# Attention output turned by VectorE block transposes and packed by SBUF transfers

## The chip, the core and the metric

The kernel runs on one core of a Trainium2 chip. The core has TensorE (PE in the profile, its weight loads PEld), VectorE (DVE), ScalarE (ACT), GpSimd (POOL) and SyncE (SP), which here issues every DMA. Each engine runs its own instruction list in order, and semaphores tie the lists together. The metric is device time of one execution in microseconds (us).

## What is computed

One transformer block on 2048 tokens of width 640, in bf16:

```python
def _A_ref(x, wqkv, wo):                       # 32 heads of 20 columns
    qkv = (x @ wqkv).reshape(B, S, 3, H, Dh).transpose(2, 0, 3, 1, 4)
    q, k, v = qkv[0], qkv[1], qkv[2]
    scores = einsum("bhqd,bhkd->bhqk", q, k) * (Dh ** -0.5)
    o = einsum("bhqk,bhkd->bhqd", softmax(scores), v)
    return o.transpose(0, 2, 1, 3).reshape(B, S, D) @ wo
def _B_ref(x, w_gate, w_up, w_down):           # Df = 1728
    return (gelu(x @ w_gate) * (x @ w_up)) @ w_down
h = x + _A_ref(layernorm(x), wqkv, wo)
out = h + _B_ref(layernorm(h), w_gate, w_up, w_down)
```

## The kernel before

**Tiles.** The scores are made as tiles of 128 keys by 512 columns of queries in PSUM, 2048 tiles in all. The four heads of one group `g` (there are eight groups) sit in the four 32-row strips of TensorE. A quad is the four heads' tiles of one place. ScalarE turns most tiles into probabilities with one exp over the two or three PSUM banks of a "unit" (`unit`, L1020; units take banks 0 to 2 and 3 to 4 in turn). VectorE makes the exps of the rest by integer arithmetic (`d_exp`, L979: four readings of a bank, L985, then four operations over the quad). `D_QUADS` (L400) says how many quads of each slot go to VectorE, 86 in all, and `D_LEAD` when. A VectorE tile gets its scores either in the third bank of a three-bank unit, which then leaves two banks to ScalarE (the slots in `DIN`, L369), or in a background bank (7 or 5). The loop at L912 to L931 cuts the tiles into units. Probabilities are kept in a ring of `PR + PR2` = 18 tiles.

**Slots and query chunks.** The queries are worked on in ranges `QR`: one of 512, six of 256, four of 128. A slot is one accumulation of P times V in PSUM bank 6, with 512 columns: one group of a 512 range, two groups of a 256 range, four of a 128 range. There are 33 slots; the first six are groups 0 to 5 of the first 512 queries, and groups 6 and 7 of these follow as two slots of 256.

**Epilogue.** At a slot's end `epilogue` (L1131) copies bank 6 to `osb` (L1137, which frees the bank), TensorE turns it with four fp32 transposes into a background bank (L1149), and VectorE takes the reciprocals of the row sums (L1156; the sum is a 21st column of V) and multiplies into `o_nat` (L1160), queries on partitions. When a query chunk has all eight groups, `post` (L1175) turns `o_nat` again into `oT` (columns on partitions): for chunks 0 to 2 (`PE_T` = 3) by five TensorE transposes per 128 queries and a VectorE copy (`transposes`, L670), for chunks 3 to 8 by a DMA transpose on SP's queue (`dma_transposes`, L686), for chunk 9, the tail, in two steps on TensorE. Then come the multiplication with `wo` (L1213), the residual (L1214), the second layernorm, written into `o_nat` and turned into `hnT`, and the gated MLP (`mms`, L1242; `down`, L1350) as background work beside the next slots.

**Order.** The program carries its own planner (`Sched`, L48). Every operation is given an engine, a duration, a latency to landing for DMAs, a priority, and its dependencies; `schedule` simulates the engines and so fixes the order of each instruction list. On the chip each list runs in exactly this order: an instruction whose semaphore is late holds all that stand behind it on its engine. The planner's costs are written beside each operation: a DMA transpose is put at 1.25 us of SP and `XP_LAT` = 4 us to landing. The `wo` multiplication has priority 1.9, behind score multiplications (0) and P times V (1), ahead of the epilogue (2) and the background (3).

Of the kernel before, what the change touches and what calls it, by code (L numbers as in the profile page):

```python
# [356 lines left out]
D = 640  # L357
# [10 lines left out]
FOUR = ()  # L368
DIN = (16, 17, 18, 20, 21, 22, 23, 24, 25, 26, 27, 28, 29, 31, 32)  # L369
PE_WARM = ((14, ()), (6, (('x', 2),)), (4, (('x', 4),)))  # L370
# [18 lines left out]
W_EARLY = 4  # L389
PE_T = 3  # L390
XP_LAT, XR_LAT, W_LAT = 4, 5, 4.0
# [3 lines left out]
P_TANH = -1  # L395
PR, PR2 = 12, 6
D_PRIO = 2
D_SPLIT = 2
D_LAG = 2
D_QUADS = (0, 1, 2, 3, 3, 2, 4, 3, 2, 2, 3, 4, 4, 0, 3, 3, 3, 3, 4, 4, 3, 3, 4, 2, 3, 2, 2, 3, 4, 3, 1, 2, 1)  # L400
D_FIRST, D_PART = 2, 0.8
D_LEAD = ((0, 0, 0, 0, 0, 0, 0, 0), (0, 12, 18, 13, 9, 15, 10, 12, 10, 12, 17, 17, 11, 22, 17, 4, 16, 10, 16, 16, 17, 8, 22, 23, 7))
T_DVE = (0, 1, 3, 5, 9, 10, 11, 12, 13, 14)
# [12 lines left out]
def bass_sequential_preLN__mha_block__glu_gated_geglu__prompt_kernel(  # L416
# [12 lines left out]
    with ExitStack() as es:  # L429
# [3 lines left out]
        def sb(name, shape, dt=BF16):  # L433
            return es.enter_context(nc.sbuf_tensor(name, shape, dt))
# [38 lines left out]
        rc = sb("rc", [128, 2, 16], FP32)  # L473
        o_nat = sb("o_nat", [128, 4, D])
        dvx = sb("dvx", [128, 2048])
# [46 lines left out]
        ka = carve(2048)  # L522
        pts2 = carve(PR2 * 512)
        zb = dvx[:, 0:1024].rearrange("p (i s) -> p i s", i=2)

# [605 lines left out]
        def epilogue(s_, bk, d_sums):  # L1131
            s = s_ % 2
            c, gs = slots[s_]
            nq = QR[c][1]
            nt = nq // 128
            nblk = len(gs) * nt
            op("dve", I("tensor_copy", osb[:, 0:128 * nblk], PS[:, 512 * 6:512 * 6 + 128 * nblk]), c_dve(128 * nblk), P_QK,  # L1137
               reads=[("O", s_)], writes=["osb"], rel=[bk], after=tuple(d_sums))
            end = s_ == len(slots) - 1
            p = P_END if end else P_EPI  # L1140
            b2 = Bank(*(ALLB if end else BGC[c]))
            key = ("bk", sc_id())
            aft = set()
            tb = rbase(c)
            for g in gs:
                for tt in range(nt):
                    aft.update(sc.rd.get(("on", g, tb + tt), ()))
            for tt in range(nblk):
                op("pe", lambda eng, tt=tt, o=128 * (tt % nt * len(gs) + tt // nt): eng.transpose(bank(b2)[:, o:o + 128],  # L1149
                                                          osb[:, tt * 128:(tt + 1) * 128], identf[:]),  # L1150
                   c_mm(128, 2.5), p, mode="full", reads=["osb", "identf"], writes=[key], acq=[b2] if tt == 0 else [],
                   after=tuple(aft) if tt == 0 else ())
# [3 lines left out]
            op("dve", lambda eng: eng.reciprocal(rcv, bv()[:, :, :, DH]), 0.17, min(p, sc.ev), reads=[key], writes=[("rc", s)])  # L1156
# [3 lines left out]
            op("dve", lambda eng: eng.tensor_tensor(  # L1160
                dst, src(), rcn.rearrange("p (t j) -> p t j", t=nt).unsqueeze(3).to_broadcast([128, nt, 4 * n, DH]), ALU.mult),
               c_dve(80 * nblk), min(p, sc.ev), reads=[key, ("rc", s)], writes=[("on", g, tb + tt) for g in gs for tt in range(nt)], rel=[b2])


        def prefetch(c):
# [9 lines left out]
        def post(c, first_banks, banks, tail):  # L1175
# [7 lines left out]
            for tt in range(tb, tb + nt):  # L1183
                t = q0 // 128 + tt - tb
                i = t % 2
                if tail:
                    for k, (a0, a1) in enumerate(((0, NA - 1), (NA - 1, NA))):
                        bk, key = Bank(*(first_banks if k else BGC[c + 1])), ("bk", sc_id())
                        on = [("on", g, tt) for g in range(NG) if 80 * g < 128 * a1 and 80 * g + 80 > 128 * a0]
                        for a in range(a0, a1):  # L1190
# [35 lines left out]
            for tt in range(tb, tb + nt):  # L1226
                t = q0 // 128 + tt - tb
                ln_apply("dve", h_sb[:, tt, :], o_nat[:, tt, :], [("on", g, tt) for g in range(NG)], t, [("h", tt, 0), ("h", tt, 1)], pd)
                if tail:
                    transposes(o_nat[:, tt, :], [("on", g, tt) for g in range(NG)], hnT[:, :, tt * 128:(tt + 1) * 128], ("hnT", tt),  # L1230
                               first_banks, p, "dve", after=first)
                else:
                    dma_transposes(o_nat[:, tt, :], [("on", g, tt) for g in range(NG)], hnT[:, :, tt * 128:(tt + 1) * 128], ("hnT", tt),
                                   after=first)
# [167 lines left out]
        ui = 0  # L1402
        for s_, (c, gs) in enumerate(slots):
            if s_ < 8:
                g = s_
# [69 lines left out]
```

## Time and profile before

| | |
|---|---|
| median of 3 runs | 864.09 us (863.56 to 864.12) |
| profiled execution, its own time | 863.64 us |
| its span, first to last instruction | 862.0 us |
| granted TensorE clock, mean | 0.996 |
| DMA over the span | 34.34 MB, 40 GB/s |
| POOL busy | 60.5 us |

The views used below are: the page's totals of each engine; groups of instructions by line and shape, with busy time and mean duration of one; the chain of work that ended last, in order of time (start, duration, what); the timeline (start, duration, engine, line, operation, output and inputs, count); the table by windows; and DMA issues with their duration on the queue (SPq) and their time to landing. L437 is a helper that many operations share; they are told apart by their tiles. `regw` and `rege` are two SBUF regions that hold different tensors at different times, `kt_all` the keys, `pts` and a part of `rege` the ring of probabilities. A group's mean duration includes a tail that the next instruction of the same engine overlaps; the step from start to start is shorter.

### The profile page before, as it was taken

To read this page: it belongs to the slowest core of one execution; us is meant where nothing else is said; L and a number is where in the kernel's file an instruction comes from. 1 tells how busy PE (TensorE), PEld (TensorE's weight loads), DVE (VectorE), ACT (ScalarE), POOL (GpSimd) and SP (SyncE) were. 2 spreads that over 40 slices of the span, in tenths; PEclk is the share of its full clock that TensorE was granted. 3 is DMA by queue.
4 is the path that set the end of the run, shared out by engine and by line. 5 is a ranking of instruction groups with operands and counts; after the bars stand their busy time and mean duration, and the time that the engine had idled before them with its cause. 6 is when DMAs were issued, how large, how long until landed. Compare 5 with 4: busy or idle time off the path is not lost.

```text
span 862.0 us, 31727 instructions
## 1 busy us (share of the span) xinstructions
PE 821.2 (95%) x14358; PEld 428.9 (50%) x14385; DVE 733.7 (85%) x1443; ACT 831.1 (96%) x822; POOL 60.5 (7%) x194
## 2 busy tenths in 40 slices
PE   7999999999999999999998999999989999999998
PEld 3443232234445444454454444445556666666777
DVE  7736779889888999878799999999798689997884
ACT  7899999999999999999999999999999999999991
POOL 6500000000030000010002000100001010010100
PEclk8999999999999999999999999999999999999999
DMA  8211112540432000010010000020101110110000
GB/s 274 80 32 53 39 48 57 151 116 24 128 106 48 2 2 24 12 17 10 25 18 17 2 10 24 18 17 2 33 19 17 35 19 5 27 26 19 11 4 25
DMA packets 38775, 34.34 MB, mean 40 GB/s; under 512 B 18261, under 2 KB 36801, under 8 KB 38641
## 3 DMA queue, kind: packets, MB, share of 16 engines
q1 hardware_dynamic: 38640, 32.32, 14.8%
q8 instruction: 113, 1.85, 0.9%
q14 instruction: 22, 0.17, 0.1%
HBM read 20.12 MB, written 8.09 MB: 33 GB/s over the span
## 4 chain that ended last, share of the span: by engine, by line
ACT 65%; PE 19%; DVE 13%; POOL 1%; issue 1%; DMA 1%; SPq 0%; POOLq 0%; ACTq 0%
ACT pts L437 42%; ACT rege L437 20%; PE ps L1044 5%; PE ps L437 3%; PE ps L1248 3%; DVE qt_all L985 3%; PE ps L1365 3%; DVE qt_all L437 2%; ACT qt_all L437 2%; PE ps L735 2%; DVE rege L985 2%; PE ps L730 1%; DVE rege L437 1%; DVE rege L1293 1%; DVE dvx L437 1%
## 5 line engine op out<-in xcount | busy, mean ns | idle before, releaser
L437 ACT ACTIVATE pts<-ps 128x1536 bf16<-128x1536 f32 (+1 forms) x480 | 549.8, 1289 | 2.7 <-PE ps L1044 2.1
L1044 PE MATMUL ps<-qt_all,kt_all 32*128 32x256 bf16 (+2 forms) x4736 | 316.4, 257 | 20.3 <-ACT pts L437 9.1
L437 ACT ACTIVATE rege<-ps 128x1536 bf16<-128x1536 f32 (+1 forms) x232 | 275.8, 1289 | 2.4 <-PE ps L437 1.5
L1044 PEld LDWEIGHTS ps<-qt_all,kt_all 32*128 32x128 bf16 x4736 | 118.0, 92 | 208.9 <-ACT pts L437 82.4
L1248 PE MATMUL ps<-rege,regw 128*128 128x256 bf16 (+1 forms) x1193 | 136.0, 251 | 2.2 <-DVE rege L985 1.0
L985 DVE TENSOR_SCALAR qt_all<-ps 128x512 int16<-128x512 f32 x176 | 118.4, 682 | 10.4 <-PE ps L1044 9.9
L985 DVE TENSOR_SCALAR rege<-ps 128x512 int16<-128x512 f32 x164 | 110.5, 683 | 19.5 <-PE ps L1044 19.0
L437 PE MATMUL ps<-pts,v_all 128*21 128x256 bf16 (+2 forms) x2656 | 119.8, 259 | 0.0
L1248 PEld LDWEIGHTS ps<-rege,regw 128*128 128x128 bf16 x1193 | 86.0, 98 | 37.1 <-issue 19.7
L437 PE MATMUL ps<-rege,v_all 128*21 128x256 bf16 (+2 forms) x1676 | 98.5, 267 | 0.2
L437 PEld LDWEIGHTS ps<-pts,v_all 128*21 128x21 bf16 x2656 | 57.9, 91 | 26.2 <-issue 21.2
L735 PE MATMUL ps<-regw 128*128 128x512 bf16 (+1 forms) x270 | 65.0, 348 | 3.3 <-issue 1.6
L1365 PE MATMUL ps<-regw,rege 128*128 128x320 bf16 x374 | 66.3, 301 | 0.7 <-DVE rege L1293 0.4
L437 PEld LDWEIGHTS ps<-rege,v_all 128*21 128x21 bf16 x1676 | 41.2, 91 | 23.6 <-issue 12.9
L437 DVE TENSOR_SCALAR qt_all<-qt_all 128x2048 int16<-128x2048 int16 (+2 forms) x103 | 47.8, 472 | 0.7
L1307 DVE SCALAR_TENSOR_TENSOR qt_all<-qt_all,ps 128x512 bf16<-128x512 f16 (+1 forms) x54 | 36.0, 667 | 12.2 <-PE ps L1248 8.2
L1365 PEld LDWEIGHTS ps<-regw,rege 128*128 128x128 bf16 x374 | 31.5, 98 | 22.5 <-issue 9.1
L437 POOL CAST mv<-mv 128x4 bf16<-128x4 f32 (+2 forms) x13 | 3.5, 271 | 545.8 <-DVE mv L437 543.5
L1293 DVE TENSOR_SCALAR rege<-ps 128x512 bf16<-128x512 f32 (+1 forms) x54 | 36.1, 668 | 5.6 <-PE ps L1248 3.4
L735 PEld LDWEIGHTS ps<-regw 128*128 128x128 bf16 x289 | 23.4, 99 | 29.9 <-issue 16.9
L437 DVE TENSOR_SCALAR rege<-rege 128x2048 int16<-128x2048 int16 x56 | 38.1, 683 | 0.3
L437 ACT ACTIVATE qt_all<-qt_all 128x512 f16<-128x512 f16 (+1 forms) x54 | 38.0, 727 | 0.0
(137 smaller groups left out, 840.6 us busy)
## 6 DMA issues: line engine op xcount, KB each, us to landing
q_rows<-regw SPq DMA_DIRECT2D x20, 128.0 KB, 2.0
out_dram<-rege SPq DMA_DIRECT2D x16, 160.0 KB, 2.7
regw<-in_A_wqkv_dram SPq DMA_DIRECT2D x3, 800.0 KB, 11.5
rege<-in_A_x_dram SPq DMA_DIRECT2D x7, 320.0 KB, 3.6
regw<-in_B_w_gate_dram SPq DMA_DIRECT2D x5, 432.0 KB, 3.4
regw<-in_B_w_up_dram SPq DMA_DIRECT2D x5, 432.0 KB, 3.4
rege<-in_A_x_dram SPq DMA_DIRECT2D x3, 640.0 KB, 6.9
kt_all<-k_rows SPq DMA_DIRECT2D x12, 160.0 KB
```

The lines of the kernel that those rows point to most:

```text
L437: return lambda eng: getattr(eng, method)(*args, **kwargs)
L730: return [lambda eng, j=j: eng.matmul(PS[32 * j:32 * j + 32, 512 * bk.b + lo:512 * bk.b + hi], l[:, 32 * j:32 * j + 32], r, start=start, s ...
L735: yield op("pe", lambda eng, l=l, r=r, k=k: eng.matmul(bank(bk, n), l, r, start=(k == 0), stop=(k == len(steps) - 1), skip_group_check=Tru ...
L985: d_ops.append(op("dve", lambda eng: eng.tensor_scalar(v[:, 512 * h:512 * h + 512], bank(b), EXP_MUL, 0.0, ALU.mult, ALU.max), c_dve(512), ...
L1044: return lambda eng: eng.matmul(out()[:, kk * nq:(kk + 1) * nq], kt_all[32 * j:32 * j + 32, g, kt * 128:(kt + 1) * 128], qt_all[32 * j:32 ...
L1248: op("pe", lambda eng, a=a, f=f, fi=fi: eng.matmul(bank(bk)[:, fi * nq:(fi + 1) * nq], w[:, a, F0[f]:F0[f] + 128], hnT[:, a, 128 * tb:128 ...
L1293: op("dve", lambda eng, bg=bg, fv=hv(k, w), w=w: eng.tensor_scalar(fv, bank(bg, w), 0.5, None, ALU.mult), c_dve(w), p, reads=[kg], writes= ...
L1307: op("dve", lambda eng, bu=bu, z=z, w=w: eng.scalar_tensor_tensor(out=z, in0=z.bitcast(F16), scalar=1.0, in1=bank(bu, w), op0=ALU.add, op1 ...
L1365: op("pe", lambda eng, f=f, o=o, hf=hf, bk=bk: eng.matmul(bank(bk, 320), ha_f[:, o:o + 128], wd[:, f, hf * 320:(hf + 1) * 320], start=(f = ...
```

## The change

In `epilogue`, for all ranges but the last of 128 queries, VectorE now reads bank 6 with a transpose in 32x32 blocks into `osb`, takes the reciprocals, multiplies into a new bf16 tile `onb`, and transposes that in blocks into the first half of `osb`, seen as bf16. Each head's 20 columns then stand on 20 partitions, and one DMA per head, from SBUF to SBUF on SP's queue, puts them at their place in `ox`, the memory of `o_nat` with the columns on partitions; a head that crosses a multiple of 128 takes two DMAs. `post` multiplies `ox` with `wo` without turning it first. The second layernorm is turned as before. `onb` takes one place of the ring of probabilities (`PR2` 6 to 5). The constants of the distribution, `D_QUADS`, `D_LEAD` and `DIN`, are new: 88 quads for VectorE, and 9 slots in `DIN` in place of 15. The planner is told `O_ISSUE` = 0.1 us of SP and `O_LAT` = 2.5 us to landing for each new DMA.

```diff
-DIN = (16, 17, 18, 20, 21, 22, 23, 24, 25, 26, 27, 28, 29, 31, 32)
+DIN = (7, 16, 22, 25, 26, 27, 28, 29, 30)
...
-PE_T = 3
+O_ISSUE, O_LAT = 0.1, 2.5
...
-PR, PR2 = 12, 6
+PR, PR2 = 12, 5
...
-D_QUADS = (0, 1, 2, 3, 3, 2, 4, 3, 2, 2, 3, 4, 4, 0, 3, 3, 3, 3, 4, 4, 3, 3, 4, 2, 3, 2, 2, 3, 4, 3, 1, 2, 1)
+D_QUADS = (0, 3, 2, 3, 3, 3, 3, 2, 2, 2, 3, 4, 3, 3, 3, 3, 3, 3, 4, 4, 2, 3, 4, 0, 4, 2, 3, 4, 2, 3, 1, 4, 0)
 D_FIRST, D_PART = 2, 0.8
-D_LEAD = ((0, 0, 0, 0, 0, 0, 0, 0), (0, 12, 18, 13, 9, 15, 10, 12, 10, 12, 17, 17, 11, 22, 17, 4, 16, 10, 16, 16, 17, 8, 22, 23, 7))
+D_LEAD = ((0, 0, 0, 0, 0, 0, 0, 0), (0, 10, 18, 12, 6, 11, 11, 18, 17, 10, 13, 16, 20, 16, 16, 5, 22, 23, 27, 7, 8, 9, 18, 30, 5))
...
-        o_nat = sb("o_nat", [128, 4, D])
+        ox = sb("ox", [128, 4 * D])
+        o_nat = ox[:, :].rearrange("p (t d) -> p t d", t=4)
...
         pts2 = carve(PR2 * 512)
+        onb = carve(512)
...
+            if c < len(QR) - 1:
+                n = len(gs)
+                w = 128 * nblk
+                o16 = osb[:, :].bitcast(BF16)
+                op("dve", I("transpose", osb[:, 0:w], PS[:, 512 * 6:512 * 6 + w]), c_dve(w), P_QK,
+                   reads=[("O", s_)], writes=["osb"], rel=[bk], after=tuple(d_sums))
+                ov = osb[:, 0:w].rearrange("p (k e) -> p k e", e=32)
+                rcn = rc[:, s, 0:w // 32]
+                op("dve", I("reciprocal", rcn, ov[:, :, DH]), 0.2, p, reads=["osb"], writes=[("rc", s)])
+                op("dve", I("tensor_tensor", onb[:, 0:w].rearrange("p (k e) -> p k e", e=32)[:, :, 0:DH], ov[:, :, 0:DH],
+                            rcn.unsqueeze(2).to_broadcast([128, w // 32, DH]), ALU.mult), c_dve(DH * w // 32), p, reads=["osb", ("rc", s)], writes=["onb"])
+                op("dve", I("transpose", o16[:, 0:w], onb[:, 0:w]), c_dve(w), p, reads=["onb"], writes=["osb"])
+                for gi, g in enumerate(gs):
+                    for j in range(4):
+                        r = 80 * g + DH * j
+                        k = 0
+                        while r < 80 * g + DH * j + DH:
+                            m = min(DH - k, 128 - r % 128)
+                            src = o16[32 * j + k:32 * j + k + m, nq * gi:nq * gi + nq]
+                            if nq > 256:
+                                dst = ox[r % 128:r % 128 + m, :].rearrange("p (u a s) -> p u a s", u=2, a=NA)[:, :, r // 128, :]
+                                src = src.rearrange("p (u s) -> p u s", u=2)
+                            else:
+                                dst = ox[r % 128:r % 128 + m, D * tb:D * (tb + nt)].rearrange("p (a s) -> p a s", a=NA)[:, r // 128, :]
+                            op("sp", I("dma_start", dst, src), O_ISSUE, P_EPI, reads=["osb"], writes=[("on", g, tb + tt, 2 * j + (k > 0)) for tt in range(nt)],
+                               sem="ot", lat=O_LAT)
+                            k += m
+                            r += m
+                return
...
-                elif c < PE_T:
-                    transposes(o_nat[:, tt, :], [("on", g, tt) for g in range(NG)], oT[:, :, tt * 128:(tt + 1) * 128],
-                               ("hnT", tt), first_banks, P_EPI, "dve", after=first)
-                else:
-                    dma_transposes(o_nat[:, tt, :], [("on", g, tt) for g in range(NG)], oT[:, :, tt * 128:(tt + 1) * 128],
-                                   ("hnT", tt), after=first)
...
-                    st = [(oT[:, a, tt * 128:(tt + 1) * 128], wo[:, a, hf * 320:(hf + 1) * 320]) for a in range(NA)]
+                    ot = oT if tail else ox[:, D * tb:D * (tb + nt)].rearrange("p (a s) -> p a s", a=NA)
+                    o = tt if tail else tt - tb
+                    st = [(ot[:, a, o * 128:(o + 1) * 128], wo[:, a, hf * 320:(hf + 1) * 320]) for a in range(NA)]
...
-                        list(chain(bk, key, 320, st, [("hnT", tt), "wo"], p, after=(sc.lw[("h", tt, hf)], *first)))
+                        list(chain(bk, key, 320, st, [k for t_ in range(tb, tb + nt) for k in onk(t_)] + ["wo"], p, after=(sc.lw[("h", tt, hf)], *first)))
...
+            if s_ == 0:
+                cst(I("memset", onb[:].bitcast(FP32), 0.0), "onb", 256, e_ops + q_first)
```

`onk(tt)` lists the keys of all eight groups and eight half-heads of one block of 128 queries, so each `wo` multiplication waits for every packing DMA of its chunk.

More of the change, by code (lines that the diff above doesn't have):

```diff
@@ L1136, in epilogue @@
             nblk = len(gs) * nt
+            end = s_ == len(slots) - 1
+            p = P_END if end else P_EPI
+            tb = rbase(c)
+            if c < len(QR) - 1:
[27 more added lines that the diff above has]
+                return
@@ L1137, in epilogue @@
             op("dve", I("tensor_copy", osb[:, 0:128 * nblk], PS[:, 512 * 6:512 * 6 + 128 * nblk]), c_dve(128 * nblk), P_QK,
                reads=[("O", s_)], writes=["osb"], rel=[bk], after=tuple(d_sums))
-            end = s_ == len(slots) - 1
-            p = P_END if end else P_EPI
             b2 = Bank(*(ALLB if end else BGC[c]))
@@ L1143, in epilogue @@
             aft = set()
-            tb = rbase(c)
             for g in gs:
                 for tt in range(nt):
-                    aft.update(sc.rd.get(("on", g, tb + tt), ()))
+                    for k in range(8):
+                        aft.update(sc.rd.get(("on", g, tb + tt, k), ()))
             for tt in range(nblk):
@@ L1161, in epilogue, with onk @@
                 dst, src(), rcn.rearrange("p (t j) -> p t j", t=nt).unsqueeze(3).to_broadcast([128, nt, 4 * n, DH]), ALU.mult),
-               c_dve(80 * nblk), min(p, sc.ev), reads=[key, ("rc", s)], writes=[("on", g, tb + tt) for g in gs for tt in range(nt)], rel=[b2])
+               c_dve(80 * nblk), min(p, sc.ev), reads=[key, ("rc", s)], writes=[("on", g, tb + tt, k) for g in gs for tt in range(nt) for k in range(8)], rel=[b2])
+        def onk(tt):
+            return [("on", g, tt, k) for g in range(NG) for k in range(8)]
         def prefetch(c):
@@ L1188, in post @@
                         bk, key = Bank(*(first_banks if k else BGC[c + 1])), ("bk", sc_id())
-                        on = [("on", g, tt) for g in range(NG) if 80 * g < 128 * a1 and 80 * g + 80 > 128 * a0]
+                        on = [("on", g, tt, k) for k in range(8) for g in range(NG) if 80 * g < 128 * a1 and 80 * g + 80 > 128 * a0]
                         for a in range(a0, a1):
@@ L1227, in post @@
                 t = q0 // 128 + tt - tb
-                ln_apply("dve", h_sb[:, tt, :], o_nat[:, tt, :], [("on", g, tt) for g in range(NG)], t, [("h", tt, 0), ("h", tt, 1)], pd)
+                ln_apply("dve", h_sb[:, tt, :], o_nat[:, tt, :], onk(tt), t, [("h", tt, 0), ("h", tt, 1)], pd)
                 if tail:
-                    transposes(o_nat[:, tt, :], [("on", g, tt) for g in range(NG)], hnT[:, :, tt * 128:(tt + 1) * 128], ("hnT", tt),
+                    transposes(o_nat[:, tt, :], onk(tt), hnT[:, :, tt * 128:(tt + 1) * 128], ("hnT", tt),
                                first_banks, p, "dve", after=first)
                 else:
-                    dma_transposes(o_nat[:, tt, :], [("on", g, tt) for g in range(NG)], hnT[:, :, tt * 128:(tt + 1) * 128], ("hnT", tt),
+                    dma_transposes(o_nat[:, tt, :], onk(tt), hnT[:, :, tt * 128:(tt + 1) * 128], ("hnT", tt),
                                    after=first)
```

## Prediction, made before the result was known

> **What bounds the kernel now.** I read the totals first, then the table by windows for the stage in which exps run, then the chain of work that ended last.
>
> ```profile
> span 862.0 us, 31727 instructions
> PE 821.2 (95%) x14358; PEld 428.9 (50%) x14385; DVE 733.7 (85%) x1443; ACT 831.1 (96%) x822; POOL 60.5 (7%) x194
> ACT 65%; PE 19%; DVE 13%; POOL 1%; issue 1%; DMA 1%; SPq 0%; POOLq 0%; ACTq 0%
> ```
>
> ```profile
> core 0: us, PE busy (x) PEld busy (x) DVE busy (x) ACT busy (x) POOL busy (x), PEclk, DMA share, GB/s
> 480.00:600.00 120.00, 115.38 (x1914) 56.80 (x1916) 118.86 (x226) 118.53 (x120) 4.25 (x14) 1.00 0.08 13
> ...
> 32.00:838.00 806.00, 773.87 (x13891) 396.62 (x13911) 697.85 (x1349) 801.55 (x766) 43.87 (x145) 1.00 0.14 34
> ```
>
> In the 806 us from the first exp to the last, ScalarE is idle for 4.45 us. So the time is ScalarE's work, with 32 us ahead of it and 24 us behind it. VectorE has 108 us of idle time there (806 - 698), though almost none between 480 and 600 (1.1 us of 120). TensorE's 774 us are pipelined and say little about room. The step of one exp is read from the chain, where consecutive pieces stand start to start (a three-bank exp takes 1.34 us, a two-bank one 0.92, a tanh of the MLP 0.51), and the counts from the groups by shape:
>
> ```profile
> 647.93 0.92 ACT rege L437
> 648.85 0.51 ACT qt_all L437
> 649.36 1.34 ACT rege L437
> ...
> L437 ACT ACTIVATE pts<-ps 128x1024 bf16<-128x1024 f32 x291 | 312.2, 1117 | 0.2 <-PE ps L437 0.2
> L437 ACT ACTIVATE pts<-ps 128x1536 bf16<-128x1536 f32 x189 | 293.6, 1554 | 2.5 <-PE ps L1044 2.1
> L437 ACT ACTIVATE rege<-ps 128x1024 bf16<-128x1024 f32 x141 | 152.1, 1117 | 1.5 <-PE ps L437 1.5
> L437 ACT ACTIVATE rege<-ps 128x1536 bf16<-128x1536 f32 x91 | 141.7, 1557 | 0.9 <-PE ps L1044 0.8
> ```
>
> That is 280 long exps (189 + 91) and 432 short ones (291 + 141), or 280 x 1.34 + 432 x 0.92 = 772.6 us; some 54 tanhs bring it near 800.
>
> **ScalarE's work.** The loop that cuts tiles into units, counted through with the old constants, gives just these 280 and 432. With the new quads, leads and `DIN` it gives 303 of three banks, 393 of two and one of a single bank (0.92 - 0.42 = 0.5 us): 406.0 + 361.6 + 0.5 = 768.1 us. ScalarE loses **4.5 us**: 3.4 us are the eight tiles of two more quads (0.42 to 0.43 each), the rest 15 fewer instructions. Since ScalarE is full, this comes off the end if nothing starves it.
>
> **TensorE and VectorE.** The rows that are removed or changed, and those that make up a quad:
>
> ```profile
> L1149 PE MATMUL ps<-identf,osb 128*128 128x128 f32 x128 | 26.2, 296 | 1.4 <-DVE rege L1293 1.0 <-DVE rege L781 0.2
> L674 PE MATMUL ps<-ident,o_nat 128*128 128x128 bf16 x35 | 3.3, 221 | 0.0
> ...
> L985 DVE TENSOR_SCALAR qt_all<-ps 128x512 int16<-128x512 f32 x176 | 118.4, 682 | 10.4 <-PE ps L1044 9.9
> L437 DVE TENSOR_SCALAR rege<-rege 128x2048 int16<-128x2048 int16 x56 | 38.1, 683 | 0.3
> L437 DVE TENSOR_TENSOR dwx<-qt_all,dwx 128x1024 bf16<-128x1024 bf16 x50 | 32.8, 678 | 0.2
> L437 DVE COPY osb<-ps 128x512 f32<-128x512 f32 x31 | 21.2, 684 | 4.1 <-PE ps L437 3.9
> L1160 DVE TENSOR_TENSOR o_nat<-ps,rc 128x320 bf16<-128x320 f32 x31 | 15.0, 484 | 0.4
> L1156 DVE RECIPROCAL rc<-ps 128x16 f32<-128x16 f32 x31 | 7.8, 251 | 6.1 <-PE ps L1149 6.1
> L683 DVE COPY rege<-ps 128x640 bf16<-128x640 bf16 x7 | 3.4, 484 | 1.4 <-PE ps L674 1.4
> ```
>
> Of the 33 slots 30 take the new path. TensorE loses 120 of the 128 fp32 transposes, 120/128 x 26.2 = 24.6 us, and 30 of the 35 small ones, 2.8 us. ScalarE waits for TensorE only in its 4 us, so I count this at nothing: room, not time.
>
> VectorE keeps a pass over bank 6 (now a transpose), the reciprocals and the multiplication, and adds a second transpose. No block transpose stands in this trace. By the nearest row, the copy of the same 512 columns, it takes 0.684 us; from below 0.42 us, by the bf16 operations on 512 columns, from above 1.37, twice the copy. I take 0.684, so 30 x 0.684 = 20.5 us are added. A quad is 4 x 0.682 + 2 x 0.683 + 2 x 0.678 = 5.45 us, two more are 10.9; six copies of 0.484 go, 2.9. VectorE gains 28.5 us against 108 idle. In the full stretch (480 to 600, slots 17 to 21) five transposes add 3.4 us, but the new `D_QUADS` has 16 quads there in place of 17, which takes 5.45 off. I count VectorE at nothing; without that cover it is a rival below. The shorter ring costs nothing by the same count of units: seven laps of 18 hold about 46 units (712 in 109 laps), of 17 about 44 (697 in 110), and ScalarE's waits for P times V are 1.7 us in all (the two "PE ps L437" above), which is the most I see this change by.
>
> **SP's queue, where the change is priced low.** The new path issues one DMA per head and a second where a head crosses a multiple of 128: 9 per slot of one or two groups, 18 per slot of four (12 once, 13 never; groups 0 to 5 of the first range make 27 in six slots). All in all 27 + 9 + 9 + 4 x 36 + 3 x 36 = 297. The planner believes 0.1 us of issue each and 2.5 us to landing. The trace has an operation of almost the same form, eight DMAs of 20 rows from SBUF to SBUF that place the keys of group 0 (`kt_all<-regw`), beside the same 20 rows fetched from DRAM:
>
> ```profile
> L437 SPq DMA_DIRECT2D kt_all<-k_rows x16: 292/330/338, 42.4 to 145.8; - x16
> L437 SPq DMA_DIRECT2D kt_all<-regw x8: 706/707/933, 22.8 to 28.2; - x8
> ...
> 22.75 6.20 SPq L437 DMA_DIRECT2D kt_all<-regw  x8
> ...
> k_rows<-regw SPq DMA_DIRECT2D x12, 128.0 KB, 1.8
> rege<-o_nat SPq DMA_TRANSPOSE x24, 2.9
> ```
>
> The columns of the first two rows are the shortest, median and longest issue in ns: 707 from SBUF to SBUF, 330 from DRAM. Eight took 6.20 us, 0.775 each. The price of the new DMAs lies between 0.1 (the planner's) and 0.775; I take 0.775, the row with the same memories on both sides and the same rows. To landing I take 1.8 us (between 1.8 and 2.9 in the rows above).
>
> The Trainium skill speaks for the change here: "DMA: Bandwidth & Descriptors", section "Issuing engines are not separate DMA queues", says that the sequencer's time to initiate a DMA is usually small relative to the DMA. By that, this part would cost nothing and the sum would be the 859 of the first rival. The row of 707 ns beside 1.8 us to landing speaks against it.
>
> **What it does to the order.** Most packing DMAs have a whole slot, some 25 us, to land. The last slot of a chunk hasn't: the chunk's `wo` multiplication waits for all of them, and in TensorE's list it stands where the planner thinks that they have landed. Before, the planner expected two DMA transposes after 2 x 1.25 + 4 = 6.5 us, one after 5.25. The trace shows `wo` that near behind them:
>
> ```profile
> 440.27 3.15 SPq L437 DMA_TRANSPOSE rege<-o_nat  x2
> 446.08 0.45 PE L735 MATMUL ps<-wo,rege 128*128 128x320 bf16 x2
> ...
> 688.36 1.21 SPq L437 DMA_TRANSPOSE rege<-o_nat  x1
> 695.40 0.57 PE L735 MATMUL ps<-wo,rege 128*128 128x320 bf16 x3
> ```
>
> So `wo` came 5.8 and 7.0 us after the first issue: 0.7 early and 1.8 late against the plan, 0.5 late on average. Now the plan expects 9 x 0.1 + 2.5 = 3.4 us for 9 DMAs and 4.3 for 18. At 0.775 the ninth is issued after 8 x 0.775 = 6.2 and lands at 8.0; the eighteenth after 13.2, landing at 15.0. `wo` waits 8.0 - 3.4 - 0.5 = **4.1 us** in six chunks (0 to 5) and 15.0 - 4.3 - 0.5 = **10.2 us** in three (6 to 8). Behind it on TensorE stand the next score multiplications, and ScalarE waits for these. It has between one short exp (0.92) and a pair (2.26) in hand, on average 1.6. It idles 2.5 us six times and 8.6 three times: 15.0 + 25.8 = **40.8 us**, which nothing makes good, because ScalarE has no slack later.
>
> **Sum.** The profiled execution took 863.64 us, 1.6 more than its span and 0.45 less than the median of the three runs. 863.6 - 4.5 + 40.8 = **900 us**. With the ends of slack and cover (1.8 and 2.26; 0 and 0.92) the idle is 6 x 0.5 + 3 x 6.6 = 23 or 6 x 3.7 + 3 x 9.8 = 52, so 882 to 911 for this case. A stall may also cost clock: between 16 and 20 us the trace grants 0.50, after a stretch in which TensorE was busy for 2.46 of 4 us.
>
> ```profile
> 12.00:16.00 4.00, 2.46 (x14) 1.22 (x15) 3.95 (x13) 3.40 (x9) 2.54 (x6) 0.66 1.07 363
> 16.00:20.00 4.00, 3.78 (x25) 2.84 (x25) 2.63 (x9) 2.12 (x5) 1.67 (x5) 0.50 0.83 280
> ```
>
> One such slice of 4 us at half clock behind each of the three long stalls is up to 2 us each; it moves the upper end to about 915. The Trainium skill, "TensorE: Matmul & The Clock Gate", Part 1, has the same halving after an idle window of about 3.4 us; by that page's window the estimate is 1.7 us each, 905 in sum.
>
> **The rivals.**
> - *The packing is hidden* (0.27): the DMAs issue fast, or land before the planner's moment, and ScalarE stays full. Then 863.6 - 4.5 = **859**, faster; 855 at best, if the 4.45 us of idle shrink because 27 us of TensorE work are gone. For it speaks that ScalarE's plan held so exactly; against it the 707 ns.
> - *The issue costs what the DRAM rows cost* (0.12): 0.33 with a gap of 0.04. Nine land after 8 x 0.37 + 1.8 = 4.8, 1.4 late, which ScalarE's reserve covers; eighteen after 8.1, 3.8 late, 1.7 us of idle after slack and cover, three times. 863.6 - 4.5 + 5.1 = **864**, no change.
> - *VectorE becomes the bound* (0.07): if a block transpose takes 1.37, the 60 of them add 30 x (0.69 + 1.37) = 62 us against 108, and in 480 to 600 five slots need 10.3 us where 1.1 + 5.45 are to be had. Some 4 us are lost there and as much in the other full slices: about **867**, slower. It decides from 1.3 us per transpose.
> - *The stalls* (0.54): **900**, the forecast.
>
> The range goes from 856 to 915. A measurement of this kernel can tell about 0.2% from no change. Faster 0.27, the same 0.12, slower 0.61.
>
> **What would show it.** Packing DMAs on SP's queue at about 0.7 us each; TensorE waiting for a DMA ahead of the first `wo` multiplication of chunks 0 to 8, about 4 us six times and 10 us three times; ScalarE idle by some 40 us between its first and last exp, in nine places, with 768 us of exps. If the new rows show 0.1 to 0.3 us, or the waits lie elsewhere, this is wrong. VectorE should show 30 x 2 transposes near 0.68 us and about 762 us busy.

## The result, and the profile after

The changed kernel takes **931.0 us** (median of 6 runs, 926.39 to 931.65), the kernel before 863.72 us (6 runs, 862.87 to 864.12). The ratio is 1.0771, with a 95% interval of 1.0749 to 1.0793: slower by 67 us. The forecast was 900 us, with a range up to 915. The sign and the kind of loss were right, the size was not.

The page's totals of the changed kernel, with the shares of the chain that ended last:

```profile
span 929.2 us, 31786 instructions
PE 830.0 (89%) x14242; PEld 422.6 (45%) x14242; DVE 753.9 (81%) x1483; ACT 829.9 (89%) x807; POOL 61.7 (7%) x195
ACT 35%; DVE 28%; PE 26%; SPq 6%; issue 2%; DMA 2%; POOL 1%; POOLq 0%; DVEq 0%; ACTq 0%
```

ScalarE has as much work as before (829.9 us against 831.1), but its share of the span falls from 96% to 89%, and in the chain ScalarE's 65% have become 35%. SP's queue, at 0% before, now holds 6% of the chain, and it is the queue of the new DMAs. VectorE's share of the chain rises too, from 13% to 28%; whether VectorE is the cause is tested in experiment 1. No engine has become fuller than ScalarE was, so the time is in waits. The table by windows says how much of it (columns: window, its length, busy time and instructions of PE, PEld, DVE, ACT and POOL, granted clock, DMA share, GB/s):

```profile
32.00:906.00 874.00, 783.40 (x13798) 391.93 (x13797) 718.27 (x1389) 799.27 (x750) 44.32 (x145) 0.96 0.13 32
217.00:232.00 15.00, 14.31 (x146) 5.44 (x146) 7.47 (x17) 10.74 (x10) 2.90 (x14) 0.80 0.08 28
360.00:372.00 12.00, 11.39 (x121) 4.17 (x120) 7.86 (x16) 8.34 (x7) 0.00 (x0) 0.59 0.01 1
740.00:748.00 8.00, 8.00 (x154) 4.97 (x152) 5.18 (x13) 3.95 (x4) 0.66 (x3) 0.67 0.02 4
799.01:802.35 3.34, 3.34 (x51) 1.97 (x52) 1.09 (x3) 0.00 (x0) 0.00 (x0) 0.50 0.02 5
```

From the first exp to the last ScalarE is idle for 874.0 - 799.27 = **74.7 us**; before it was 4.45. The phase is 68 us longer, the span 67.2. So the whole loss lies between the first and the last exp, and it is idle time of ScalarE. The other four rows are stretches behind waits of TensorE, and they come up again below: TensorE is busy in nearly all of each, at a granted clock of 0.50 to 0.80, and ScalarE still has gaps (in the last row it has not started again).

The new operations, in the tables by tile and by shape (DMA rows: shortest, median and longest time on the queue in ns):

```profile
L437 SPq DMA_DIRECT2D ox<-osb x297: 554/707/1337, 66.5 to 860.4; - x149
```

```profile
L437 ACT ACTIVATE pts<-ps 128x1536 bf16<-128x1536 f32 x199 | 303.5, 1525 | 11.9 <-PE ps L1046 11.6
L437 ACT ACTIVATE rege<-ps 128x1536 bf16<-128x1536 f32 x104 | 158.8, 1527 | 17.9 <-PE ps L1046 17.3 <-PE ps L437 0.3
L437 DVE STREAM_TRANSPOSE osb<-ps 128x512 f32<-128x512 f32 x30 | 21.3, 709 | 6.0 <-PE ps L437 4.6 <-PE ps L732 1.4
L437 DVE STREAM_TRANSPOSE osb<-rege 128x512 bf16<-128x512 bf16 x30 | 21.0, 701 | 0.0
```

There are 297 packing DMAs at a median of 707 ns of SP's queue, 303 exps of three banks (199 + 104), and 60 block transposes at 0.70 us, all as counted. The waits of TensorE by line (us in total, times, longest), with SP's queue and `wo` (L732 and L737) in them:

```profile
PE ps L737 <- DMA ox<-osb: 22.5, 4, 9.7
PE ps L737 <- issue: 12.4, 2, 8.7
PE ps L732 <- DMA ox<-osb: 10.0, 1, 10.0
PE ps L1279 <- DMA rege<-ox: 8.9, 2, 8.0
```

The first three rows are `wo` behind its packing DMAs. (The "issue" of the second row is no other cause: its 8.7 us end at 739.5, just after SP has issued the last packing DMA of chunk 6 at 738.3.) The last row isn't `wo`. It is the up and gate multiplication of the MLP, waiting for the second layernorm's DMA transposes, and the forecast doesn't have it. On ScalarE the stalls look so (timeline of ScalarE; in brackets the idle time ahead of the instruction):

```profile
219.77 1.45 ACT L437 ACTIVATE rege<-ps 128x1536 bf16<-128x1536 f32 x1 [5.62 <-PE ps L1046]
223.73 5.55 ACT L437 ACTIVATE pts<-ps 128x1024 bf16<-128x1024 f32 x5 [1.17 <-PE ps L1046]
...
256.23 1.02 ACT L437 ACTIVATE rege<-ps 128x1024 bf16<-128x1024 f32 x1 [3.27 <-PE ps L1046]
360.04 1.02 ACT L437 ACTIVATE rege<-ps 128x1024 bf16<-128x1024 f32 x1 [1.27 <-PE ps L1046]
362.29 2.52 ACT L437 ACTIVATE pts<-ps 128x1536 bf16<-128x1536 f32 x2 [1.23 <-PE ps L1046]
...
466.12 1.02 ACT L437 ACTIVATE pts<-ps 128x1024 bf16<-128x1024 f32 x1 [4.28 <-PE ps L1046]
568.88 1.45 ACT L437 ACTIVATE pts<-ps 128x1536 bf16<-128x1536 f32 x1 [4.81 <-PE ps L1046]
...
709.15 1.45 ACT L437 ACTIVATE rege<-ps 128x1536 bf16<-128x1536 f32 x1 [8.23 <-PE ps L1046]
742.01 1.02 ACT L437 ACTIVATE rege<-ps 128x1024 bf16<-128x1024 f32 x1 [8.80 <-PE ps L1046]
744.38 1.45 ACT L437 ACTIVATE rege<-ps 128x1536 bf16<-128x1536 f32 x1 [1.34 <-PE ps L1046]
802.35 1.02 ACT L437 ACTIVATE pts<-ps 128x1024 bf16<-128x1024 f32 x1 [11.05 <-PE ps L1046]
...
863.26 1.02 ACT L437 ACTIVATE pts<-ps 128x1024 bf16<-128x1024 f32 x1 [9.97 <-PE ps L1046]
```

This gives the account of the 74.7 us:

| place | ScalarE idle, us | forecast |
|---|---|---|
| `wo` of chunks 0 to 4 (5.62, 3.27, 1.27, 4.28, 4.81); chunk 5 shows none | 19.3 | 15.0 |
| `wo` of chunks 6 to 8 (8.80, 11.05, 9.97) | 29.8 | 25.8 |
| the layernorm's transposes of chunk 5, at 709 | 8.2 | not in it |
| eight gaps of 0.9 to 1.3 in the 10 us behind the stalls (1.17, 1.23 and 1.34 above) | 9.3 | in the upper end only |
| all the rest (4.5 before the change) | 8.1 | 4.5 |
| sum | 74.7 | 45.3 |

One long `wo` stall (chunk 7) and the stall that was not forecast, in the timeline of all engines:

```profile
690.38 13.28 SPq L437 DMA_DIRECT2D ox<-osb  x18
692.49 0.81 DVE L437 TENSOR_SCALAR ox<-rege,mu,rs 128x640 bf16<-128x640 bf16 x2
703.70 2.57 SPq L437 DMA_TRANSPOSE rege<-ox  x2
707.77 0.80 PE L1279 MATMUL ps<-rege,regw 128*128 128x256 bf16 x3 [8.04 <-DMA rege<-ox]
...
784.64 13.23 SPq L437 DMA_DIRECT2D ox<-osb  x18
...
799.01 1.52 PE L737 MATMUL ps<-wo,ox 128*128 128x320 bf16 x5 [9.74 <-DMA ox<-osb]
800.73 0.61 PE L437 MATMUL ps<-qt_all,v_all 128*21 128x128 bf16 x16
801.12 0.64 PE L437 MATMUL ps<-dvx,v_all 128*21 128x128 bf16 x16
801.69 0.61 PE L1046 MATMUL ps<-qt_all,kt_all 32*128 32x128 bf16 x12
```

At 784.64 the eighteen DMAs of the chunk's last slot start and hold SP for 13.23 us, 0.735 each. TensorE stands at `wo` from 789.3, 4.6 us after the first issue, to 799.01. At 692.5 it is another queue: the layernorm of chunk 5 is ready by 693.3, but its two DMA transposes stand on SP behind the 18 packing DMAs of chunk 6's first slot. They start at 703.70, and the MLP that waits for them holds up TensorE and, by 8.23 us, ScalarE.

### The profile page after: what moved, and what is told of

It reads as the page before. It is cut to its first block, busy times and chain, and to the rows that moved or that the text cites. A ratio compares the mean times of both kernels' runs of the same rounds, so it can differ in the third digit from the quotient of the medians.

```text
span 929.2 us, 31786 instructions
## 1 busy us (share of the span) xinstructions
PE 830.0 (89%) x14242; PEld 422.6 (45%) x14242; DVE 753.9 (81%) x1483; ACT 829.9 (89%) x807; POOL 61.7 (7%) x195
## 4 chain that ended last, share of the span: by engine, by line
ACT 35%; DVE 28%; PE 26%; SPq 6%; issue 2%; DMA 2%; POOL 1%; POOLq 0%; DVEq 0%; ACTq 0%
ACT pts L437 23%; ACT rege L437 11%; PE ps L1046 7%; DVE qt_all L987 6%; SPq L437 6%; PE ps L437 5%; DVE qt_all L437 5%; PE ps L737 4%; PE ps L1279 4%; DVE rege L437 3%; DVE dvx L987 3%; PE ps L1396 3%; DVE dwx L437 3%; DVE osb L437 2%; DVE rege L1324 2%
## 5 line engine op out<-in xcount | busy, mean ns | idle before, releaser
L1046 PE MATMUL ps<-qt_all,kt_all 32*128 32x256 bf16 (+2 forms) x4736 | 323.6, 261 | 25.2 <-ACT pts L437 6.8
L437 ACT ACTIVATE rege<-ps 128x1536 bf16<-128x1536 f32 (+1 forms) x220 | 268.2, 1303 | 32.2 <-PE ps L1046 31.7
L1279 PE MATMUL ps<-rege,regw 128*128 128x256 bf16 (+1 forms) x1179 | 136.7, 253 | 12.5 <-DMA rege<-ox 8.9
L1279 PEld LDWEIGHTS ps<-rege,regw 128*128 128x128 bf16 x1179 | 86.1, 98 | 51.8 <-issue 30.3
L987 DVE TENSOR_SCALAR dvx<-ps 128x512 int16<-128x512 f32 x100 | 67.3, 680 | 8.4 <-PE ps L1046 8.0
L737 PE MATMUL ps<-regw 128*128 128x512 bf16 (+1 forms) x297 | 70.5, 350 | 1.4 <-DVE regw L685 0.9
L737 PE MATMUL ps<-wo,ox 128*128 128x320 bf16 x130 | 32.9, 386 | 37.9 <-DMA ox<-osb 22.5
L1245 DVE TENSOR_TENSOR rege<-ps,rege 128x320 bf16<-128x320 f32 x32 | 15.4, 486 | 60.5 <-PE ps L737 56.2
L1396 PE MATMUL ps<-regw,rege 128*128 128x320 bf16 x350 | 63.1, 302 | 0.8 <-DVE dvx L987 0.8
L987 DVE TENSOR_SCALAR rege<-ps 128x512 int16<-128x512 f32 x72 | 48.5, 681 | 7.4 <-PE ps L1046 7.0
L437 DVE TENSOR_SCALAR qt_all<-qt_all 128x512 f16<-128x512 f16 (+2 forms) x111 | 52.6, 484 | 0.4
L1396 PEld LDWEIGHTS ps<-regw,rege 128*128 128x128 bf16 x350 | 28.2, 98 | 22.4 <-issue 8.2
```

Of the source, the lines that this page charges most:

```text
L437: return lambda eng: getattr(eng, method)(*args, **kwargs)
L737: yield op("pe", lambda eng, l=l, r=r, k=k: eng.matmul(bank(bk, n), l, r, start=(k == 0), stop=(k == len(steps) - 1), skip_group_check=Tru ...
L987: d_ops.append(op("dve", lambda eng: eng.tensor_scalar(v[:, 512 * h:512 * h + 512], bank(b), EXP_MUL, 0.0, ALU.mult, ALU.max), c_dve(512), ...
L1046: return lambda eng: eng.matmul(out()[:, kk * nq:(kk + 1) * nq], kt_all[32 * j:32 * j + 32, g, kt * 128:(kt + 1) * 128], qt_all[32 * j:32 ...
L1279: op("pe", lambda eng, a=a, f=f, fi=fi: eng.matmul(bank(bk)[:, fi * nq:(fi + 1) * nq], w[:, a, F0[f]:F0[f] + 128], hnT[:, a, 128 * tb:128 ...
L1396: op("pe", lambda eng, f=f, o=o, hf=hf, bk=bk: eng.matmul(bank(bk, 320), ha_f[:, o:o + 128], wd[:, f, hf * 320:(hf + 1) * 320], start=(f = ...
```

## The experiments

The theory after the result: the time is lost because the planner is told 0.1 us for a DMA that holds SP's queue for 0.71 us, and so puts `wo` and the layernorm's consumers too early. The rival causes are the block transposes on VectorE, a landing time that is too long whatever the planner knows, and the new constants. Each kernel was timed beside the kernel before, whose medians were 863.4 to 863.7 us. In the edits that follow, everything else is as in the changed kernel unless said otherwise.

**1. Tell the planner the issue.**

```diff
-O_ISSUE, O_LAT = 0.1, 2.5
+O_ISSUE, O_LAT = 0.75, 2.5
```

> The changed kernel with one constant altered: the planner is told 0.75 us of SP per packing DMA in place of 0.1. Theory A (the loss is the order: `wo` and the layernorm's transposes stand too early in the lists, because each packing DMA holds SP for 0.71 us): the waits of TensorE for ox shrink below 1 us each, ScalarE's idle time between its first and last exp falls from 75 us to 5 to 14, and the time is 859 to 869 us. Theory B (the loss is the work itself, 297 small transfers and some 20 us more of VectorE): telling the planner only moves the waits, and the time stays above 900.

868.26 us (866.84 to 869.26), ratio 1.0054 (1.0039 to 1.0069). One number that only the planner reads takes away 63 of the 67 us; the same DMAs and the same transposes run.

```profile
32.00:838.00 806.00, 760.92 (x13779) 384.50 (x13801) 717.11 (x1381) 797.39 (x750) 48.36 (x146) 1.00 0.13 35
```

In that kernel's table by windows ScalarE is idle for 8.6 us of 806 (7.1 between its first and last exp) and the clock is 1.00. VectorE has as much work as in the changed kernel (717 us against 718 in the two windows) and yet the 63 us are gone, so it isn't their cause.

**2. Tell only a late landing**, which keeps `wo` away from the DMAs but says nothing of the queue.

```diff
-O_ISSUE, O_LAT = 0.1, 2.5
+O_ISSUE, O_LAT = 0.1, 13.0
```

> The changed kernel with the planner told 13 us to landing and still 0.1 us of SP. This parts two mechanisms of theory A. The stalls ahead of wo (49 us) should go, since 13 + 0.9 or 1.8 us covers 8 and 15 us nearly; the layernorm's DMA transposes still stand behind packing DMAs that hold SP for 7 to 13 us, so one or more stalls of 3 to 8 us on rege<-ox stay: 866 to 880 us. If SP's queue is no cause of its own, it ends within 3 us of the first of these runs.

879.79 us (two runs, 879.44 and 880.14), ratio 1.0189 (1.0168 to 1.0209): at the upper edge. The waits of `wo` for `ox` are gone from TensorE's list, and of its waits for a DMA these are left:

```profile
PE ps L732 <- DMA rege<-ox: 4.9, 1, 4.9
PE ps L1279 <- DMA rege<-ox: 2.9, 1, 2.9
```

Both are DMA transposes of the layernorm behind packing DMAs on SP. So there are two mechanisms, `wo` behind its DMAs and other transfers behind the same DMAs, and the difference between 879.8 and 868.3 is about what the second costs when only the first is cured. The traces bear this out: between the first and the last exp ScalarE is idle for 18.1 us here and for 7.1 in experiment 1, and the stretch behind the last exp is as long in both (30.7 and 30.8 us).

**3. Old epilogue for the ranges of 128** (chunks 6 to 8, eighteen DMAs a slot), the new one for the others, `O_ISSUE` still 0.1.

```diff
-            if c < len(QR) - 1:
+            if c < 7:
...
+                if not tail and c >= 6:
+                    dma_transposes(o_nat[:, tt, :], onk(tt), oT[:, :, tt * 128:(tt + 1) * 128], ("hnT", tt), after=first)
```

> The changed kernel, but the six slots of the 128-query ranges 7 to 9 go the old way (fp32 transposes on TensorE, DMA transposes for chunks 6 to 8). Theory A: the three long stalls ahead of wo (8.8, 11.1, 10.0 us), the 8.2 us behind the 18 DMAs of the first such slot and some 2.6 us after them are gone, 40.7 us in all: 890 us (884 to 896). Theory B, a loss that goes by slots: 6 of 30 slots are taken out of about 71 us, 14 us: 917.

893.37 us (two runs, 891.61 and 895.13), ratio 1.0346 (1.0319 to 1.0373). In its timeline the four long stalls (8.23, 8.80, 11.05 and 9.97, together 38.1 us) don't occur, and the early ones stand as they were:

```profile
220.67 1.45 ACT L437 ACTIVATE rege<-ps 128x1536 bf16<-128x1536 f32 x1 [5.16 <-PE ps L1046]
256.26 1.02 ACT L437 ACTIVATE rege<-ps 128x1024 bf16<-128x1024 f32 x1 [3.26 <-PE ps L1046]
465.58 1.02 ACT L437 ACTIVATE pts<-ps 128x1024 bf16<-128x1024 f32 x1 [4.41 <-PE ps L1046]
567.70 1.45 ACT L437 ACTIVATE pts<-ps 128x1536 bf16<-128x1536 f32 x1 [4.45 <-PE ps L1046]
```

The time falls by 37.6 us, within the expected range, so the eighteen-DMA slots carry the long stalls, the one at 709 included. That 37.6 comes so close to 38.1 is in part luck: ScalarE's idle time falls by 43.6 us (from 74.7 to 31.1), with some of the smaller gaps gone as well, and the stretch behind the last exp grows by 3.8 us.

**4. The constants alone**, in the kernel before: new `DIN`, `D_QUADS` and `D_LEAD`, and `PR2` = 5, with the old epilogue.

> The kernel before with the new D_QUADS, D_LEAD, DIN and the ring of 17 alone, epilogue and post as before. The prediction's term of -4.5 us by itself: 303 long and 393 short exps, ScalarE's idle time about 4 to 6 us, 859.6 us (858 to 861.5). Against it: the two more quads and the nine slots of DIN were chosen for a VectorE and TensorE load that this kernel hasn't got; then ScalarE idles more and the time is 864 or above.

886.3 us (885.05 to 888.13), ratio 1.0265 (1.0246 to 1.0284): a miss for the term of -4.5 us. The other case, 864 or above with ScalarE idling more, came true, by far more than was thought. The page's span is 885.1 us, and the timeline shows a stall that neither kernel has:

```profile
137.04 7.43 PE L730 MATMUL ps<-regw 128*32 128x320 bf16 x160
...
144.83 1.02 ACT L437 ACTIVATE rege<-ps 128x1024 bf16<-128x1024 f32 x1 [11.47 <-PE ps L1044]
```

ScalarE loses 11.47 us at 145, while TensorE has narrow multiplications on the weights and no scores, and 40.8 us lie behind the last exp in place of 23.7. The constants belong to the order that they were chosen for, and in the old order they can't be priced. The next pair prices them inside the new order.

**5. Issue and landing told, with the new and with the old constants.**

```diff
-O_ISSUE, O_LAT = 0.1, 2.5
+O_ISSUE, O_LAT = 0.75, 1.35
```

> As the run with 0.75 us of SP told (868.3), with the landing told at 1.35 us after the issue in place of 2.5, since the packing DMAs landed about 2.05 us after their issue began (0.71 + 1.35). Theory A: 1.1 us less between a chunk's last packing DMA and its wo; that counts only behind the last exp, where chunk 8 is late: 865 to 868, stalls ahead of wo still below 1.5 us each. If the stalls come back (wo waiting over 2 us for ox), the landing was read too short.

> The same planner costs (0.75 and 1.35 us), but D_QUADS, D_LEAD and DIN as before the change (86 quads): the new path alone, planned rightly. Theory A with the prediction's term: ScalarE has 4.5 us more of exps, so it ends 3 to 6 us behind the run with the new constants, 868 to 873. Against it: VectorE's 21 us of second transposes are what binds; then 86 quads (11 us less of VectorE) are as fast or faster, 862 to 867.

867.6 us (865.68 to 868.5), ratio 1.0043 (1.0028 to 1.0058), with the new constants; 870.69 us (869.55 to 875.08), ratio 1.0091 (1.0065 to 1.0118), with the old `DIN`, `D_QUADS` and `D_LEAD`. Both lie in the ranges expected by theory A. The new constants are worth 3.1 us. The table by windows for the first of the two, then for the second:

```profile
31.30:833.30 802.00, 759.83 (x13797) 381.99 (x13821) 711.90 (x1373) 796.25 (x748) 46.94 (x146) 1.00 0.14 35
...
833.30:864.00 30.70, 27.63 (x366) 22.72 (x363) 16.01 (x44) 11.36 (x16) 0.00 (x0) 1.00 0.05 18
```

```profile
31.70:840.00 808.30, 754.15 (x13660) 378.92 (x13687) 706.45 (x1364) 801.56 (x764) 47.82 (x146) 1.00 0.14 35
840.00:867.60 27.60, 23.43 (x371) 19.20 (x359) 13.61 (x38) 6.49 (x11) 0.00 (x0) 1.00 0.06 20
```

With the new constants the exps take 802.0 us in place of the 806.0 of the kernel before and start 0.9 us earlier, yet the span is 2.0 us longer, since behind the last exp there are 30.7 us in place of 23.7. With the old constants the exps take 808.3 us and 27.6 us follow: the new ones save 6.3 us of exps, and 3.1 of these come back behind the last exp. Here are the multiplications of the MLP in that stretch, the tail, first for the kernel before (groups by line, from 838 us on), then for the told kernel with the new constants (from 833 us on):

```profile
L1365 PE MATMUL ps<-regw,rege 128*128 128x320 bf16 x70 | 10.2, 299 | 0.0
L1248 PE MATMUL ps<-rege,regw 128*128 128x128 bf16 x148 | 8.8, 219 | 0.0
```

```profile
L1279 PE MATMUL ps<-rege,regw 128*128 128x128 bf16 x239 | 14.6, 219 | 0.2 <-DVE rege L1401 0.2
...
L1396 PE MATMUL ps<-regw,rege 128*128 128x320 bf16 x84 | 12.1, 299 | 0.0
```

L1248 and L1279 are the same up and gate multiplications, L1365 and L1396 the same down multiplications. 26.7 us of them are left in place of 19.0: 7.7 us more, against a tail that is 7.0 longer. TensorE is busy for 27.6 of the 30.7 us, so it is what bounds the tail, and work that the old order did beside the exps is left over in the new one. (With the old constants 20.8 us of these multiplications are left.)

**6. Is it because chunk 8 is late?** In the kernel before, the layernorm transpose of chunk 8 stands on SP at 809.0, 29 us ahead of the last exp, in the told kernel of experiment 5 at 821.0, 12 us ahead of it. Two kernels take chunk 8, or all chunks from 6 on, back to the old epilogue, both with 0.75 and 1.35 told (the edit of experiment 3, with `c < 9` and with `c < 7`).

> The run with both costs told (867.6), but the two slots of the last 128-query range ahead of the tail, which feed chunk 8, go the old way; the other 28 the new way. Theory A2: what is left against the forecast of 859 is the tail: after the last exp 30.7 us pass in place of 23.7, because chunk 8's wo can't start before 18 packing DMAs have been issued and landed (15 us), so more of its MLP stands behind the last exp. The old way takes about 7 us there: the stretch behind the last exp falls to 23 to 26 us, and the time to 859 to 863. If VectorE's load or the new constants make the tail long, it stays above 865.

> Both costs told; all six slots of 128-query ranges go the old way, the 24 of the larger ranges the new way. The same tail as with chunk 8 alone on the old way, 4 us less of VectorE and 108 packing DMAs fewer, but 24 fp32 transposes back on TensorE: 858 to 863 by theory A2, and the issue of 0.71 us then costs nothing measurable; above 865 if the constants bind.

870.35 us (870.13 to 872.79), ratio 1.0085 (1.007 to 1.01), and 871.64 us (869.32 to 872.06), ratio 1.0088 (1.0073 to 1.0103): both misses for theory A2, and above the 865 that was named for a tail made by VectorE's load or the constants. With chunk 8 the old way its transpose starts at 814.4, 23 us ahead of the last exp, and still 230 up and gate multiplications are left, and 33.5 us of tail (35.3 in the other). The lateness shrinks and the tail grows, so late packing isn't what fills it. The constants are part of the answer (experiment 7 says how much); why the planner leaves the rest of the background behind there stays open.

**7. A cheaper issue.** The packing goes through DRAM: four DMAs per slot write 20 rows each, for all groups of the slot, to a DRAM tensor, and one DMA per chunk fetches them into `ox`.

```diff
-O_ISSUE, O_LAT = 0.1, 2.5
+O_ISSUE, O_LAT, O_LOAD = 0.36, 1.7, 2.4
...
+                for j in range(4):
+                    op("sp", I("dma_start", rows[j, :, gs[0]:gs[-1] + 1, q0:q0 + nq], o16[32 * j:32 * j + DH, 0:n * nq].rearrange("p (g s) -> p g s", g=n)),
...
+                if gs[-1] == NG - 1:
+                    op("sp", I("dma_start", ox[:, D * tb:D * (tb + nt)].rearrange("p (a s) -> p a s", a=NA),
+                               our.rearrange("(a p) s -> p a s", p=128)[:, :, q0:q0 + nq]), O_ISSUE, P_EPI,
```

> VectorE's two transposes kept, the packing done otherwise: four DMAs per slot from SBUF to rows in DRAM (one per strip of 20 rows, all groups at once), and one DMA per chunk from there into ox; 30 x 4 + 9 = 129 DMAs in place of 297. If the 0.71 us belong to copies from SBUF to SBUF, these show 0.32 to 0.36 us each as the other DMAs with DRAM on one side do, SP is held for 45 us in place of 210, wo stands 6 us behind the last transpose in all chunks (before the run with told costs: 8 and 15), and chunk 8 isn't late any more: 857 to 863. If the 0.71 us come from the 20 rows, the issues show about 0.7 again and the time stays at 864 or above.

> The same packing through DRAM with D_QUADS, D_LEAD and DIN of before (86 quads). The term of -4.5 us in the other direction: 861 to 867, 3 to 6 us behind the same with the new constants; as fast or faster if VectorE's load binds.

867.27 us (865.15 to 870.04), ratio 1.0041 (1.0021 to 1.0062); with the old constants 871.68 us (870.77 to 872.93), ratio 1.0095 (1.0079 to 1.011). Both times are misses: the told kernel stayed above 864 although the price of an issue fell. That price is as expected (table by tile, columns as above):

```profile
L437 SPq DMA_DIRECT2D o_rows<-osb x120: 273/336/1472, 67.6 to 794.2; - x120
L437 SPq DMA_DIRECT2D ox<-o_rows x9: 382/387/391, 213.5 to 795.6; - x9
```

The same 20 partitions cost 336 ns on SP when they go to DRAM, and 707 when they go to SBUF. So on SP's queue it is the pair of memories that costs, not the rows, as with the keys in the kernel before (330 from DRAM, 707 from SBUF, to the same tile). Once the planner knows the price, the two ways can't be told apart by their time: 867.3 against 867.6. The old constants cost 4.4 us here. Again the new ones shorten the exps (808.2 us against 816.1) and lengthen the tail (26.0 against 23.0). So the new constants come with a longer tail in all three pairs: 40.8 against 23.7 us in the kernel before (experiment 4), 30.7 against 27.6 told, 26.0 against 23.0 through DRAM. They shorten the exps and leave more of the background behind them: some 3 of the 7 us by which the tail of experiment 5 is longer are theirs.

**8. Two queues.** As in experiment 5, with the odd heads' DMAs issued by GpSimd (told 1.0 and 2.0).

```diff
-                            op("sp", I("dma_start", dst, src), O_ISSUE, P_EPI, reads=["osb"], writes=[("on", g, tb + tt, 2 * j + (k > 0)) for tt in range(nt)],
-                               sem="ot", lat=O_LAT)
+                            op(("sp", "pool")[j % 2], I("dma_start", dst, src), (O_ISSUE, 1.0)[j % 2], P_EPI, reads=["osb"], writes=[("on", g, tb + tt, 2 * j + (k > 0)) for tt in range(nt)],
+                               sem=("ot", "op")[j % 2], lat=(O_LAT, 2.0)[j % 2])
```

> Both costs told; every second head's packing DMA is issued by GpSimd in place of SP (told 1.0 us each and 2.0 to landing), so a chunk's last 18 go out over two queues. By theory A2 what counts is when the last one lands: at about 0.7 on SP and 1 us on GpSimd it is 9 to 11 us in place of 15, so the tail shrinks by 3 to 5 us: 862 to 866. If GpSimd takes over 1.5 us for each, its queue is late where the planner thinks otherwise and stalls ahead of wo come back: 870 or more.

869.61 us (867.43 to 871.37), ratio 1.0077 (1.006 to 1.0094): a miss, though GpSimd takes far less than the 1.5 us at which stalls were expected. The table by tile:

```profile
L437 POOL DMA_DIRECT2D ox<-osb x149: 502/516/1027, 67.2 to 793.2; - x149
L437 SPq DMA_DIRECT2D ox<-osb x148: 559/707/1462, 66.9 to 793.6; - x148
```

GpSimd takes 516 ns for the same DMA. Half the load on SP brings nothing more, which speaks against SP's queue as the bound of the told kernels. No version beat the kernel before.

## Why the prediction was wrong in size and right in kind

- **ScalarE bounds the time; a stall there is not made good.** Right: 70.2 us more idle in the phase (74.7 - 4.45), 67.2 us more span.
- **ScalarE's work falls by 4.5 us.** Right in the phase from first to last exp, about: the counts are 303 and 393, and the phase of experiment 5 is 4.0 us shorter than before; by the constants alone it shrinks by 6.3 and 7.9 us in the two pairs of experiments 5 and 7. (In the changed kernel the rows show 2.3 us less busy time, 801.55 - 799.27.) The other half of that step, that it "comes off the end if nothing starves it", failed even where nothing starved: 7.0 us of tail came back, as 7.7 us of MLP multiplications. The forecast's 32 us ahead and 24 us behind were treated as fixed, but the tail holds what the phase leaves over. No version reached the first rival's 859: with the issue told, the best is 867.
- **VectorE has room.** Right: 709 and 701 ns per block transpose where 684 was taken, 753.9 us busy where 762 were expected; experiment 1 runs them at no loss.
- **0.775 us of SP per DMA, from the row of the same memories.** Right: 0.735 in a full queue of eighteen. The row from DRAM would have misled by a factor of two here, as experiment 7 shows (336 against 707). The Trainium skill, "DMA: Bandwidth & Descriptors", section "Issuing engines are not separate DMA queues", calls the sequencer's time usually small relative to the DMA; for these small copies the trace disagrees, with 13.23 us of issue and 1.14 us from there to the `wo` that waited.
- **The step that failed is "What it does to the order": 40.8 us of added idle time, measured 70.2 (74.7 - 4.45).** Three terms of it.
  - *The places that it names* hold 49.1 us in place of 40.8. TensorE's waits were near what was worked out in the three long places (8.70, 9.74 and 10.02 us against 10.2); of the six short ones, put at 4.1 each, five came (4.87, 3.74, 2.39, 4.28 and 3.64) and chunk 5 had none. In sum that is 47.4 us against 55.2, so the waits came out too long, not too short. What was put at nothing is ScalarE's loss behind the wait. The forecast took 1.6 us of cover off and added nothing. But `wo` has to run itself, and in chunk 7 two groups of P times V stood behind it before the next scores: from 799.01 to the exp at 802.35 pass 3.34 us. ScalarE had run on for 2.0 us after TensorE stopped, and 9.74 + 3.34 - 2.0 is the 11.05 of the row. Over the eight places the times from the start of `wo` to ScalarE's next exp are 16.3 us, and the cover is 14.6, 1.8 each: 47.4 + 16.3 - 14.6 = 49.1. So the waits, put 7.8 us too long, hid a part of the 16.3 us that were left out.
  - *A queue that it did not follow*: 8.2 us. It counted what SP's 13 us do to `wo`, but not to the other users of SP. The layernorm's transposes sat in the same queue (the row at 703.70), and experiment 2 shows this as a loss of its own.
  - *The clock behind a stall*: 9.3 us, which stood in the range's upper end only, and only for the three long stalls. The rows by windows show 0.80, 0.59 and 0.67 for 8 to 15 us, and `wo` took a median of 424 ns in place of 299; in experiment 1, without the stalls, the clock is 1.00 and `wo` takes 299 again. The short stalls had it too: 6.7 of the 9.3 us lie behind the stalls of chunks 0 to 4. That the gaps come from the clock is read from the trace, since no run changes the clock alone: seven of the eight begin while it is 0.50. The 3.34 us of chunk 7 ran at 0.50 as well (the last row by windows), so a part of the first term also belongs here. The Trainium skill, "TensorE: Matmul & The Clock Gate", Part 1, agrees in kind; the forecast's 1.7 us per long stall by that page is near the gaps of 1.2 to 1.3 us that stand behind two of them.
- **The range** ended at 915 because its ends moved only the terms already in the sum and a small one for the clock (three times up to 2 us on top of 911 is 917, not 915, which would not have reached 931 either). The 16.3 and 8.2 us and most of the 9.3 were in no case. That 900 was not further off is in part luck, since the waits were put too long.

## What to carry to other kernels

Where a planner fixes the order, an operation's told price is part of the kernel: a DMA told at 0.1 us that holds its queue for 0.7 cost 63 us here, and the same transfers, told at 0.75, lost none of it. When many small DMAs go to a queue, follow every later user of that queue, not only their consumer, and price a stall from the wait to the next instruction of the bounding engine, with the work in between. A saving on the bounding engine comes off the end only if the background that ran beside it still fits, so look at what is left behind its last instruction.

## What the runs showed of the hardware

- A copy of 20 partitions holds SP's queue for 707 ns from SBUF to SBUF, whether it is 5 or 10 KB (the 27 of the first six slots, mostly 20 KB, take 768), and for 336 ns from SBUF to DRAM with 20 KB. GpSimd issues those from SBUF to SBUF in 516 ns.
- VectorE's block transpose of 128x512 takes nearly the same time in fp32 from PSUM (709 ns) and in bf16 from SBUF (701 ns).
- Behind waits of TensorE of 4.87, 2.39 and 8.70 us the granted clock is 0.80 over 15 us, 0.59 over 12 and 0.67 over 8, although TensorE is busy in over 94% of these stretches. The shortest of these waits, 2.39 us, was followed by the halved clock; one of 2.29 us, in experiment 6 with chunk 8 the old way, was not (1.00 from 733 to 745 us).
